# Keeping two more pairs' v on the core in a sorted-block attention followed by a bilinear feed-forward

## The chip, the cores and the metric

The kernel runs on one core of one Trainium2 chip. The metric is the device time of one execution in microseconds. A core has a matrix engine (TensorE, PE in the profile; its weight loads are PEld), VectorE (DVE), ScalarE (ACT), GpSimd (POOL) and SyncE (SP), and 16 DMA engines that move data between DRAM and the on-chip memory. Each engine has its own queue of instructions and works through it in order; they wait for each other through semaphores, which a framework sets from the data dependences. Matrix products land in PSUM, from where VectorE or ScalarE copies them on.

## The reference

The inputs are q, k, v of shape 4 x 8 x 768 x 64 (batch, head, position, head dimension), an 8 x 8 sorting matrix per head, and the three weights of a feed-forward block.

```python
P = sort_net                       # 5 rounds: softmax over rows, then columns divided by their sums
k_sorted = einsum('bhij,bhjcd->bhicd', P, k_b)      # k in 8 blocks of 96 positions
v_sorted = einsum('bhij,bhjcd->bhicd', P, v_b)
scores = scale * q_b @ k_sorted^T  # each block attends to its own sorted block
attn = softmax(scores)
x = (attn @ v_sorted) -> (3072 tokens, 512)
out = ((x @ w_a) * (x @ w_b)) @ w_out               # 512 -> 1536 -> 512
```

The softmax is computed without the subtraction of the maximum, and its sum comes from a column of ones beside v.

## The kernel before

The work is cut into 16 **pairs** g of two heads, four for each batch. A pair goes through these steps:

- **C**: q is transposed on TensorE (`stage_q`, line 173, for the first two batches) or by a DMA (`q_by_dma`); k is mixed with the sorting matrix (`stage_mix`, 12 matmuls, line 186) and copied out of PSUM by ScalarE into one of five buffers kT; v is mixed.
- **R**: the scores of both halves of the blocks (line 234) and their exponentials on ScalarE (eT, line 240).
- **O**: the output matmuls `o_ps` from eT and the sorted v in `vs` (line 262), a reciprocal and a multiplication on VectorE (rec, line 266, and xp, line 268), and a transposing DMA of xp into xT, the input of the feed-forward (`to_xT_dma`, line 294).

v can go two ways. The pairs of batch 0 use `stage_mix` for v, two copies into a buffer vT (`evac_v`), eight transposes on TensorE and one copy into vs (`stage_v`, lines 248 and 250). All other pairs use `stage_v_natural`: two matmuls (line 202), one copy by VectorE (vn, line 161), a write of vn to DRAM (vd, line 208), and later `read_v`, which reads it back into vs in the other order of axes (line 212). vs has three buffers, pair g uses number g mod 3.

The feed-forward of a batch is a list of 72 **slots**: 48 of the products with w_a and w_b (`ffn_mm`, four matmuls of 384 columns, line 306; the results are copied by ScalarE, line 315, and multiplied by VectorE into hT, line 323), then 24 of the output product (`ffn_out`, three matmuls of 512 columns, line 339; every fourth one copies the result to o_sb and sends it out by two DMAs, line 346). The accumulators of the feed-forward rotate through three PSUM banks.

The steps of the pairs of batch b are hung between the slots of the batch ahead of it: `after[s]` lists what is issued behind slot s. The order on TensorE, SP and GpSimd is the order of the program; on ScalarE and VectorE the framework orders the instructions of the main loop itself. For batch 1 the list holds, before:

| pair | C | read of v | R | O |
|---|---|---|---|---|
| 4 | 21 | 27 | 29 | 34 |
| 5 | 31 | 37 | 39 | 44 |
| 6 | 41 | 47 | 49 | 54 |
| 7 | 51 | 57 | 59 | 64 |

From pair 8 on C, read, R and O stand at slots 72(b-1) + 15hp + (-4, 2, 8, 14), hp being the pair's number in its batch.

The loads of k, v and q of pair g + 3 are issued by GpSimd in step C of pair g (`load_pair`, lines 90 and 94), into rings of three buffers, so that each takes the place of pair g's. In the C step of pair 4 the last two thirds of w_out are loaded too. The writes and reads of v, the transposing DMAs and the output's DMAs are all issued by SP, in one queue.

Of the kernel before, what the change touches and what calls it, by code (L numbers as in the profile page):

```python
# [22 lines left out]
def kernel(  # L23
# [11 lines left out]
    nc = tc.nc  # L35
    P = 128
    B, H, S, D = q.shape
# [3 lines left out]
    DMODEL = H * D  # L41
# [5 lines left out]
    HP = H // 2  # L47
# [29 lines left out]


    BD = 2
    BV = 1  # L80

    def load_pair(g):
        b, hp = divmod(g, HP)
# [73 lines left out]
    def copy(eng, out, in_):  # L157
        if eng is nc.scalar:
            nc.scalar.copy(out=out, in_=in_)  # L159
        else:  # L160
            eng.tensor_copy(out=out, in_=in_)  # L161
# [35 lines left out]
    def stage_v_natural(g, pool, tag, eng):  # L197


        mix = pool.tile([P, 2, 512], FP32, tag=tag, name="mix")  # L200
        for e in range(2):
            nc.tensor.matmul(mix[:, e, 0:W], lhsT=s_all[:, 2 * g + e].rearrange("p i c -> p (i c)"),  # L202
                             rhs=loaded[g][1][:, e], start=True, stop=True)
        vn = att.tile([P, NCH, 2, D], BF16, tag="vn", name="vn")
        copy(eng, vn.rearrange("p c e d -> p e c d"),
             _ap(mix, 0, [[1024, P], [512, 2], [D, NCH], [1, D]]))
        vd = drp.tile([P, NCH * 2 * D], BF16, tag="vd", name="vd")
        nc.sync.dma_start(out=vd, in_=vn.rearrange("p c e d -> p (c e d)"))
        st[g, "vd"] = vd
# [6 lines left out]
    def evac_k_natural(g, eng):  # L216
        copy(eng, _ap(kTs[g % NKV], 0, [[S + PAD, P], [NCH, P], [1, NCH]]),
             _ap(st[g, "k"], 0, [[1024, P], [1, P], [P, NCH]]))

    def evac_k(g, eng):  # L220
        copy(eng, _ap(kTs[g % NKV], 0, [[S + PAD, P], [CG, NCH], [BLK, NB], [1, CG]]),
             _ap(st[g, "k"], 0, [[1024, P], [P, NCH], [CG, NB], [1, CG]]))

    def evac_v(g, eng, h):
        copy(eng, _ap(vTs[g % NKV], h * HK, [[2 * HK, P], [CG, NCH], [BLK, NBH], [1, CG]]),
             _ap(st[g, "v"], h * NBH * CG, [[1024, P], [P, NCH], [CG, NBH], [1, CG]]))

    def stage_scores(g, pool, tag, h):
        kT, qT, eT = kTs[g % NKV], st[g, "qT"], eTs[g % NBUF]
        sc = pool.tile([P, 2, 512], FP32, tag=tag, name="sc")  # L230
        for i in range(NBH):
            for e in range(2):
                blk = h * NBH + i
                nc.tensor.matmul(  # L234
                    sc[:, e, i * BLK:(i + 1) * BLK],
                    lhsT=kT[e * D:(e + 1) * D, blk * BLK:blk * BLK + P],
                    rhs=(qT[e * D:(e + 1) * D, blk] if g < BD * HP else
                         qT[e * D:(e + 1) * D, :, blk * CG:(blk + 1) * CG]),
                    start=True, stop=True)
        nc.scalar.activation(out=eT[:, h, :, 0:HB], in_=sc[0:BLK, :, 0:HB],  # L240
                             func=AF.Exp, scale=float(scale))
# [50 lines left out]
    def to_xT_dma(g):  # L292
        xT = xT_of(g // HP)
        nc.sync.dma_start_transpose(
            out=_ap(xT, g % HP * S, [[KA * S, P], [BLK, NB], [1, BLK]]),
            in_=st[g, "xp"].rearrange("q i e d -> q (i e d)"))
# [35 lines left out]
    def ffn_out(b, t, c, part, pool):  # L332
        hT = hTs[b]
        c0 = t * HW + c * P
        if part == 0:
            st[b, t, c] = pool.tile([P, DMODEL], FP32, tag="F", name="po")
        po = st[b, t, c]
        for m in range(part * KO // NPO, (part + 1) * KO // NPO):
            nc.tensor.matmul(po, lhsT=hT[:, m, c0:c0 + P], rhs=w_out_sb[:, m, :],  # L339
                             start=(m == 0), stop=(m == KO - 1))  # L340
        if part < NPO - 1:
            return
        o_sb = ffp.tile([P, DMODEL], FP32, tag="o_sb", name="o_sb", bufs=6)
        copy(nc.scalar if c % 2 == 0 else nc.vector, o_sb, po)
        for u in range(2):
            nc.sync.dma_start(
                out=_ap(out, (b * S + t * NBH * BLK + 2 * c + u) * DMODEL,
                        [[NCH * DMODEL, NBH * CG], [1, DMODEL]]),
                in_=o_sb[u * NBH * CG:(u + 1) * NBH * CG])
# [18 lines left out]
    with tc.manual_schedule(engines={mybir.EngineType.PE, mybir.EngineType.SP,  # L368
# [3 lines left out]
        with tc.manual_schedule(engines=fast), \  # L372
# [7 lines left out]
            for it in range(5):  # L380
# [9 lines left out]
                if it == 0:  # L390
                    with nc.allow_low_precision("sum of one one and zeros"):
                        nc.vector.reduce_sum(
                            out=mask, in_=_ap(ident, 0, [[P, P], [1, CG], [CG, NB]]), axis=AX.X)
# [43 lines left out]
        with tc.tile_pool(name="psA", bufs=2, space=PSUM) as psA, \  # L437
                tc.tile_pool(name="psB", bufs=1, space=PSUM) as psB, \
                tc.tile_pool(name="psF", bufs=3, space=PSUM) as psF:
            def Q1(g):  # L440
                stage_q(g, psA, "A", nc.vector, 1)

            def S1(g):
                stage_scores(g, psA, "A", 1)

            def V1(g):
                stage_v(g, psB, "B", 1)

            def O1(g):
                stage_o(g, psA, "A", 1)  # L450

            def X1(g):
                to_xT(g, psB, "B", 1, nc.vector)

            def C(g):
                if g < BD * HP:
                    stage_q(g, psB, "B", nc.vector)
                stage_mix(g, "k", psA, "A")
                evac_k_natural(g, nc.scalar)
                stage_v_natural(g, psA, "A", nc.vector)  # L460
                if g + 3 < B * HP:
                    load_pair(g + 3)
                if g == BV * HP:
                    for c in range(1, 3):
                        load_out(c)

            def R(g):
                stage_scores(g, psA, "A", 0)
                stage_scores(g, psA, "A", 1)

            def O(g):
                stage_o(g, psA, "A", 0)
                stage_o(g, psA, "A", 1)
                to_xT_dma(g)

            with tc.manual_schedule(engines=fast):
                g = HP - 1
                parts = {}
                for n_, (m, w_sb) in enumerate(((0, w_a_sb), (0, w_b_sb), (1, w_a_sb))):
                    parts[m, w_sb is w_b_sb] = ffn_mm(0, m, 0, w_sb, psF, 0, KA - 1)  # L480
                    if n_ == 0:
                        stage_o(g, psA, "A", 0)
                to_xT(g, psB, "B", 0, nc.vector)
                Q1(0)

            second = {0: [(Q1, 1)], 2: [(S1, 0)], 3: [(V1, 0)], 4: [(S1, 1)],
                      5: [(O1, 0), (V1, 1)], 6: [(Q1, 2)], 7: [(X1, 0)], 8: [(S1, 2), (O1, 1)],
                      9: [(V1, 2)], 10: [(Q1, 3)], 11: [(X1, 1)], 12: [(S1, 3), (O1, 2)],
                      13: [(V1, 3)], 14: [(X1, 2)], 15: [(O1, 3)], 17: [(X1, 3)]}

            NSL = 4 * KO + 2 * 3 * NPO
            after = {s: [] for s in range(-NSL, B * NSL)}
            for s, u in second.items():
                after[s] += u
            for g in range(HP, B * HP):
                b, hp = divmod(g, HP)
                r = (b - 1) * NSL + (29 + 10 * hp if b == 1 else 8 + 15 * hp)
                c_, o_ = r - (8 if b == 1 else 12), r + (5 if b == 1 else 6)
                if b >= BD:
                    after[c_ - 4].append((q_by_dma, g))  # L500
                after[c_ + 6].append((read_v, g))
                after[c_].append((C, g))
                after[r].append((R, g))
                after[o_].append((O, g))
            s = 0
            for b in range(B):
                steps = []
                for m, t in ([(m, t) for t in range(2) for m in range(KO)] if b == 0 else
                             [(m, t) for m in range(KO) for t in range(2)]):
                    for f, u in ((ffn_a, False), (ffn_b, True)):  # L510
                        pf = parts.pop((m, u), None) if (b, t) == (0, 0) else None
                        steps.append(lambda f=f, m=m, t=t, b=b, pf=pf: f(b, m, t, psF, pf))
                for t in range(2):
                    for c in range(3):
                        for part in range(NPO):
                            steps.append(lambda t=t, c=c, part=part, b=b:
                                         ffn_out(b, t, c, part, psF))
                for step in steps:
                    step()
                    for f, g in after[s]:  # L520
                        f(g)
                    s += 1
# [29 lines left out]
```

## Time and profile before

| | |
|---|---|
| median of 3 runs | 259.35 us (259.15 to 260.0) |
| profiled execution | 258.78 us |
| its span, first to last instruction | 257.0 us |
| mean granted clock of TensorE | 0.987 |
| TensorE busy | 239.6 us (93%) |
| VectorE busy | 114.5 us (45%) |
| ScalarE busy | 97.9 us (38%) |
| GpSimd busy | 55.9 us (22%) |

In the groups of the profile a line gives the line of the kernel, the engine, the operation, output and inputs with their shapes and the count; behind the bar stand the busy time in us and the mean duration in ns, and behind the second bar the idle time of the engine just ahead of these instructions with what ended it. In the list of waits a line gives who waited, for whom, the total in us, the number of waits and the longest. In the chain of waits in order of time, and in the timeline, a line begins with the start in us and the duration; the chain names what set the end at each moment. vs_116, vs_117 and vs_118 are the three buffers of vs, used by pairs 0, 3, 6, ..., by 1, 4, 7, ... and by 2, 5, 8, ...

### The profile page before, as it was taken

How to read it: one execution, taken by the hardware profiler on the slowest of the kernel's cores; microseconds unless marked ns; L12 is line 12 of the kernel's file. 1: busy time of each engine (PE TensorE's matmuls, PEld its weight loads, DVE VectorE, ACT ScalarE, POOL GpSimd, SP SyncE). 2: the span in 40 equal slices, each digit the busy share in tenths (PEclk: the TensorE clock that was granted, in tenths of full speed). 3: DMA queues.
4: the chain of work that ended last, by engine and by line, in shares of the span. 5: the costliest groups of instructions: out<-in, count | busy, mean ns of one | idle time of the engine just before them, and what ended most of it. 6: DMA issues, size and time to landing. Idle time of an engine off the chain costs nothing.

```text
span 257.0 us, 5119 instructions
## 1 busy us (share of the span) xinstructions
PE 239.6 (93%) x2068; PEld 135.8 (53%) x2081; DVE 114.5 (45%) x260; ACT 97.9 (38%) x176; POOL 55.9 (22%) x75
## 2 busy tenths in 40 slices
PE   8888999974999879999999999999999999999992
PEld 3465665642555345656564455656555466655440
DVE  6766676542365052565471233746443134444110
ACT  3484542450433413635543135462623043333010
POOL 8494383540044013304040040000000000000000
PEclk9999999996899999999999999999999999999999
DMA  6999998799298949995968599152553520000243
GB/s 90 197 203 203 203 201 128 112 181 152 61 137 119 209 112 187 130 173 74 158 101 126 117 141 195 39 87 72 53 93 86 132 59 3 0 0 3 50 113 82
DMA packets 60247, 29.44 MB, mean 115 GB/s; under 512 B 39744, under 2 KB 57152, under 8 KB 60224
## 3 DMA queue, kind: packets, MB, share of 16 engines
q0 software_dynamic: 29200, 14.16, 43.8%
q1 hardware_dynamic: 31024, 14.96, 29.7%
q8 instruction: 16, 0.26, 0.4%
q14 instruction: 7, 0.06, 0.1%
HBM read 30.68 MB, written 8.65 MB: 153 GB/s over the span
## 4 chain that ended last, share of the span: by engine, by line
PE 77%; DMA 10%; DVE 2%; issue 1%; ACT 0%; SPq 0%
PE pf L306 46%; PE po L339 21%; DMA vs_117<-vd 5%; DMA vd<-vn 4%; PE o_ps L262 3%; PE sc L234 2%; PE mix L202 2%; PE mix L186 2%; PE q_ps L173 1%; DVE vn L161 1%; PE xt_ps L287 1%; PE vs_ps L248 0%; DVE xp L268 0%; ACT o_sb L159 0%; DVE hT L323 0%
## 5 line engine op out<-in xcount | busy, mean ns | idle before, releaser
L323 DVE TENSOR_TENSOR hT<-a_sb,pf 128x384 bf16<-128x384 bf16 x96 | 53.2, 554 | 67.8 <-PE pf L306 55.8
L306 PE MATMUL pf<-xT,w_a_sb 128*128 128x384 bf16 x384 | 79.3, 329 | 0.8 <-DVE xT L161 0.7
L306 PE MATMUL pf<-xT,w_b_sb 128*128 128x384 bf16 x384 | 79.7, 330 | 0.0
L315 ACT CAST a_sb<-pf 128x384 bf16<-128x384 f32 x96 | 46.0, 479 | 82.4 <-DVE hT L323 50.2
L339 PE MATMUL po<-w_out_sb,hT 128*128 128x512 bf16 x276 | 63.0, 379 | 0.6 <-issue 0.2
L306 PEld LDWEIGHTS <-w_a_sb 128*128 128x128 bf16 x384 | 37.0, 99 | 25.0 <-issue 2.0
L306 PEld LDWEIGHTS <-w_b_sb 128*128 128x128 bf16 x384 | 36.6, 99 | 23.7 <-issue 1.0
L339 PEld LDWEIGHTS <-hT 128*128 128x128 bf16 x288 | 27.6, 98 | 31.7
L159 ACT COPY o_sb<-po 128x512 f32<-128x512 f32 x16 | 9.4, 586 | 44.1 <-PE po L339 38.7
L268 DVE TENSOR_TENSOR xp<-o_ps,rec 96x512 bf16<-96x512 f32 x32 | 21.7, 684 | 0.7
L161 DVE COPY o_sb<-po 128x512 f32<-128x512 f32 x8 | 5.5, 686 | 29.3 <-PE po L339 25.6
L266 DVE RECIPROCAL rec<-o_ps 96x8 f32<-96x8 f32 x32 | 6.1, 197 | 24.0 <-PE o_ps L262 22.8
L161 DVE CAST vn<-mix 128x768 bf16<-128x768 f32 x12 | 11.5, 956 | 4.4 <-PE mix L202 4.2
L262 PE MATMUL o_ps<-vs_117,eT_114 96*128 96x65 bf16 x80 | 4.0, 204 | 7.4 <-DMA vs_117<-vd 7.4
L365 PE MATMUL w_ps<-warm_sb 128*128 128x512 bf16 x32 | 9.4, 448 | 1.4 <-DVE warm_sb L71 1.2
L240 ACT ACTIVATE eT_113<-sc 96x768 bf16<-96x768 f32 x12 | 9.3, 805 | 3.3 <-PE sc L234 3.2
L240 ACT ACTIVATE eT_115<-sc 96x768 bf16<-96x768 f32 x10 | 7.6, 805 | 1.4 <-PE sc L234 1.4
L262 PEld LDWEIGHTS <-eT_114 96*128 96x128 bf16 x80 | 3.4, 104 | 8.7 <-DMA vs_117<-vd 5.6
L240 ACT ACTIVATE eT_114<-sc 96x768 bf16<-96x768 f32 x10 | 7.6, 806 | 0.9 <-PE sc L234 0.9
L355 POOL TENSOR_TENSOR s_all<-mask,p_col 128x1024 bf16<-128x1024 bf16 (+1 forms) x5 | 7.2, 1457 | 3.4 <-ACT p_col L408 3.4
L365 PEld LDWEIGHTS <-warm_sb 128*128 128x128 bf16 x33 | 3.3, 111 | 5.6 <-issue 2.5
L161 DVE COPY qT<-q_ps 128x384 bf16<-128x384 bf16 (+1 forms) x8 | 3.6, 453 | 3.5 <-PE q_ps L173 3.4
(192 smaller groups left out, 161.5 us busy)
## 6 DMA issues: line engine op xcount, KB each, us to landing
out_dram<-o_sb SPq DMA_DIRECT2D x48, 128.0 KB, 2.4
vd<-vn SPq DMA_DIRECT2D x12, 192.0 KB, 4.6
w_a_sb<-in_moe_w_a_dram POOLq DMA_DIRECT2D x4, 384.0 KB, 9.7
w_b_sb<-in_moe_w_b_dram POOLq DMA_DIRECT2D x4, 384.0 KB, 11.1
w_out_sb<-in_moe_w_out_dram POOLq DMA_DIRECT2D x3, 512.0 KB, 7.9
q_first<-in_q_dram POOLq DMA_DIRECT2D x2, 384.0 KB, 6.0
vs_117<-vd SPq DMA_DIRECT2D x4, 192.0 KB, 4.1
vs_118<-vd SPq DMA_DIRECT2D x4, 192.0 KB, 3.8
```

The lines of the kernel that those rows point to most:

```text
L159: nc.scalar.copy(out=out, in_=in_)
L161: eng.tensor_copy(out=out, in_=in_)
L240: nc.scalar.activation(out=eT[:, h, :, 0:HB], in_=sc[0:BLK, :, 0:HB], func=AF.Exp, scale=float(scale))
L262: nc.tensor.matmul(o_ps[:, e, i * (D + 1):(i + 1) * (D + 1)], lhsT=eT[:, h, e, i * BLK:i * BLK + P], rhs=vs[:, h * NBH + i, e * (D + 1):(e ...
L266: nc.vector.reciprocal(out=rec, in_=_ap(o_ps, 0, [[1024, BLK], [512 + D, 2], [D + 1, NBH]]))
L268: nc.vector.tensor_tensor(out=_ap(xp, h * NBH * 2 * D, [[NB * 2 * D, BLK], [D, 2], [2 * D, NBH], [1, D]]), in0=_ap(o_ps, 1, [[1024, BLK], ...
L306: nc.tensor.matmul(pf[:, 0:HW], lhsT=w_sb[:, kc, m * P:(m + 1) * P], rhs=xTs[b][:, kc, t * HW:(t + 1) * HW], start=(kc == 0), stop=(kc == ...
L315: nc.scalar.copy(out=a_sb, in_=pf[:, 0:HW])
L323: nc.vector.tensor_tensor(out=_ap(hTs[b], m * S + t * HW, [[KO * S, P], [CG, NBH], [NBH * CG, NCH], [1, CG]]), in0=st[b, m, t].rearrange(" ...
L339: nc.tensor.matmul(po, lhsT=hT[:, m, c0:c0 + P], rhs=w_out_sb[:, m, :], start=(m == 0), stop=(m == KO - 1))
L355: eng.tensor_tensor(out=s_all[:, h0:h0 + n], in0=_ap(mask, 0, [[CG, P], [0, n], [0, NB], [1, CG]]), in1=_ap(src, h0, [[NB * BH, P], [1, n] ...
L365: nc.tensor.matmul(w_ps[:, 0:cols], lhsT=warm_sb[:, 0:P], rhs=warm_sb[:, 0:cols], start=True, stop=True)
```

## The change

Three things change.

1. Pairs 4 and 5 take v the way that batch 0 does (mixing, two copies to vT by VectorE, eight transposes in step R, one copy to vs); `GV = 6` is the first pair whose v goes through DRAM. Their k is copied to kT in the other order of columns, to fit. The slots of the four pairs of batch 1 are now written out one by one:

| pair | C | read of v | R | O |
|---|---|---|---|---|
| 4 | 22 | none | 27 | 32 |
| 5 | 30 | none | 36 | 41 |
| 6 | 34 | 42 | 47 | 53 |
| 7 | 39 | 49 | 55 | 62 |

The slots of pairs 8 to 15 stay as they were.

2. The loads of pairs 8 to 15 stand in the program behind step O of pair g instead of in its step C. The load of pair 7 and of w_out stays in the C step of pair 4.

3. The very last output tile is copied out of PSUM in two halves of 256 columns, one by ScalarE, one by VectorE, instead of whole by ScalarE.

```diff
-    BV = 1
+    GV = 6
...
-        copy(nc.scalar if c % 2 == 0 else nc.vector, o_sb, po)
+        if (b, t, c) == (B - 1, 1, 2):
+            nc.scalar.copy(out=o_sb[:, 0:DMODEL // 2], in_=po[:, 0:DMODEL // 2])
+            nc.vector.tensor_copy(out=o_sb[:, DMODEL // 2:], in_=po[:, DMODEL // 2:])
+        else:
+            copy(nc.scalar if c % 2 == 0 else nc.vector, o_sb, po)
...
                 stage_mix(g, "k", psA, "A")
-                evac_k_natural(g, nc.scalar)
-                stage_v_natural(g, psA, "A", nc.vector)
-                if g + 3 < B * HP:
+                if g >= GV:
+                    evac_k_natural(g, nc.scalar)
+                    stage_v_natural(g, psA, "A", nc.vector)
+                else:
+                    evac_k(g, nc.scalar)
+                    stage_mix(g, "v", psA, "A")
+                    for h in range(2):
+                        evac_v(g, nc.vector, h)
+                if g == HP:
                     load_pair(g + 3)
-                if g == BV * HP:
                     for c in range(1, 3):
                         load_out(c)
...
                 stage_scores(g, psA, "A", 1)
+                if g < GV:
+                    stage_v(g, psB, "B")
...
                 to_xT_dma(g)
+                if HP < g < B * HP - 3:
+                    load_pair(g + 3)
...
-                r = (b - 1) * NSL + (29 + 10 * hp if b == 1 else 8 + 15 * hp)
-                c_, o_ = r - (8 if b == 1 else 12), r + (5 if b == 1 else 6)
+                if b == 1:
+                    c_, v_, r, o_ = ((22, 0, 27, 32), (30, 0, 36, 41), (34, 42, 47, 53),
+                                     (39, 49, 55, 62))[hp]
+                else:
+                    c_, v_, r, o_ = ((b - 1) * NSL + 15 * hp + u for u in (-4, 2, 8, 14))
...
-                after[c_ + 6].append((read_v, g))
+                if g >= GV:
+                    after[v_].append((read_v, g))
```

## The prediction

> **What bounds the kernel now.** I read the page's head first, then the waits of TensorE, then the chain of waits in order of time, then the busy time of two stretches.
>
> The engines' row, TensorE's waits and the page's clock row:
>
> ```profile
> span 257.0 us, 5119 instructions
> PE 239.6 (93%) x2068; PEld 135.8 (53%) x2081; DVE 114.5 (45%) x260; ACT 97.9 (38%) x176; POOL 55.9 (22%) x75
> PEclk9999999996899999999999999999999999999999
> PE o_ps L262 <- DMA vs_117<-vd: 7.4, 2, 5.2
> PE w_ps L365 <- DVE warm_sb L71: 1.2, 1, 1.2
> ```
>
> TensorE (PE) is the bound at 93%. Of its waits one group counts: the output matmuls of stage o (line 262) wait twice for v to come back from DRAM, 7.4 us together; the next one, 1.2 us, is at the start. Two slices of the clock row fall to 6 and 8 tenths. The chain shows where the two waits are:
>
> ```profile
> 45.11 0.34 PE mix L186 x12
> 45.45 0.45 PE mix L202 x2
> ...
> 46.90 4.81 DMA vd<-vn
> ...
> 51.79 9.46 DMA vs_117<-vd
> ...
> 61.29 1.06 PE o_ps L262 x16
> 62.35 5.30 PE pf L306 x20
> 67.65 0.45 PE sc L234 x16
> ...
> 70.73 1.95 PE pf L306 x12
> 72.68 0.52 PE o_ps L262 x16
> ...
> 80.54 6.14 DMA vd<-vn
> ...
> 86.73 4.39 DMA vs_117<-vd
> ...
> 143.28 5.83 PE po L339 x27
> ```
>
> A slot of the main loop is four matmuls pf or three po: 1.95 / 3 = 0.65 us, and 5.83 / 9 the same. The first trip is that of pair 4 (write 4.81 us, read 9.46 us), the second that of pair 7 (6.14 and 4.39). Behind the first wait 20 matmuls of the feed-forward take 5.30 us, where 12 take 1.95 later: 0.27 against 0.16 us each, so the clock is gone too. Busy time by stretch (columns: stretch, length, PE, PE loads, DVE, ACT, POOL, granted clock, DMA share, GB/s):
>
> ```profile
> 56.10:61.29 5.19, 0.00 (x1) 0.00 (x0) 0.01 (x1) 0.48 (x1) 0.96 (x2) 0.83 1.28 210
> 61.29:66.39 5.10, 5.10 (x30) 2.90 (x31) 2.24 (x6) 0.48 (x1) 0.00 (x0) 0.50 0.57 45
> 88.00:91.26 3.26, 1.01 (x6) 0.30 (x4) 0.00 (x0) 0.59 (x1) 0.00 (x0) 1.00 1.15 298
> ```
>
> PE stands still for 5.19 us, then works 5.10 us at half clock. The second idle time, 3.26 - 1.01 = 2.25 us, costs no clock.
>
> **Pairs 4 and 5 without DRAM.** Pair 4's wait cannot be there any more: its v never leaves the core. Gone: 5.19 us of idle time and, as half-clock work is worth half its time, 5.10 x 0.5 = 2.55 us.
>
> What comes in its place, per pair: the mixing matmuls of v like those of k (12, 0.34 us) instead of the two natural ones (0.45): -0.11. Then eight transposes in stage R, at the rate of the row below, 0.22 us for four: +0.44. For two pairs: 2 x (0.44 - 0.11) = **+0.66 us** on PE, which has no idle time left there to hide it in.
>
> ```profile
> 33.97 0.22 PE vs_ps L248 x4
> ```
>
> A rule of the Trainium skill speaks against this: its page TensorE: Matmul & The Clock Gate, Part 4, gives about 275 ns for one 128x128 transpose in a kernel, as such a transpose does not get the full clock. By that, an estimate from the page, 16 transposes would be 4.4 us instead of 0.9 and the gain some 3.5 us smaller. The row has 0.055 us each in the same kernel between the same matmuls, so I keep it.
>
> **VectorE and ScalarE.** Durations (busy, mean ns):
>
> ```profile
> L323 DVE TENSOR_TENSOR hT<-a_sb,pf 128x384 bf16<-128x384 bf16 x96 | 53.2, 554 | 67.8 <-PE pf L306 55.8 <-ACT a_sb L315 6.2 <-ACT eT_115 L240 2.6
> L268 DVE TENSOR_TENSOR xp<-o_ps,rec 96x512 bf16<-96x512 f32 x32 | 21.7, 684 | 0.7
> L161 DVE CAST vn<-mix 128x768 bf16<-128x768 f32 x12 | 11.5, 956 | 4.4 <-PE mix L202 4.2
> L266 DVE RECIPROCAL rec<-o_ps 96x8 f32<-96x8 f32 x32 | 6.1, 197 | 24.0 <-PE o_ps L262 22.8 <-issue 1.2
> L161 DVE COPY qT<-q_ps 128x768 bf16<-128x768 bf16 x4 | 2.2, 553 | 3.0 <-PE q_ps L173 3.0
> L250 DVE COPY vs_116<-vs_ps 96x512 bf16<-96x512 bf16 x4 | 1.7, 415 | 0.0
> L161 DVE CAST vT_109<-mix 128x384 bf16<-128x384 f32 x1 | 0.6, 558 | 0.0
> L159 ACT CAST kT_103<-mix 128x768 bf16<-128x768 f32 x4 | 3.2, 799 | 1.3 <-PE mix L186 1.3
> 32.00:38.00 6.00, 6.00 (x80) 3.71 (x78) 4.21 (x11) 2.85 (x5) 5.05 (x4) 1.00 1.31 200
> ```
>
> The k evacuation changes its order but not its size; the row's four, pairs 0, 5, 10 and 15, have both orders and one mean of 799 ns: 0. VectorE gets two halves of vT (2 x 0.558) for one vn (0.956), and one vs copy of double width (between 0.415 and 0.83; I take 0.83): +0.99 us a pair.
>
> That matters because the four pairs now stand closer. From the C step of pair 4 (slot 22) to the O step of pair 5 (slot 41) PE does 20 slots of 0.65 us (13.0), four C steps (two of 0.46 + 0.34 + 0.34, two of 0.46 + 0.34 + 0.45; 0.46 is the row of the q transposes below), two R steps (0.45 + 0.44) and two O steps (0.52): 20.6 us. VectorE has in it 10 hT (5.5), 4 qT (2.2), 4 vT (2.2), 2 vs (1.7), 2 vn (1.9) and 4 of rec and xp (3.5): 17.0 us, a share of 83%. The densest stretch of 6 us shown above has 4.21 of 6 (70%), with PE never idle. I followed the queue slot by slot with these durations: hT is at most 1.5 us late (behind O of pair 4), and three PSUM buffers for the feed-forward cover about that. I charge **+0.2 us**; bounds 0 and 3.8 (below).
>
> **Pair 6: the next thing that can be late.** Its v still goes through DRAM. The read is issued by SP, whose queue is in order: write of pair 6, write of pair 7, transpose of pair 5's xp, read of pair 6, read of pair 7. So the read cannot start before pair 5's O step is through VectorE, although its place is only one slot behind that. Before, the order around pair 6's read was the same:
>
> ```profile
> 72.52 0.68 PE L262 MATMUL o_ps<-vs_118,eT_115 96*128 96x65 bf16 x16
> 75.14 1.23 SPq L294 DMA_TRANSPOSE xT<-xp  x1
> 76.52 0.47 SPq L212 DMA_DIRECT2D vs_116<-vd  x1
> 81.30 0.68 PE L262 MATMUL o_ps<-vs_116,eT_113 96*128 96x65 bf16 x16
> DMA to landing us min/median/max: 3.5/3.9/4.1
> 69.51 0.46 PE q_ps L173 x12
> ```
>
> The read was issued 76.52 - 72.52 = 4.0 us after pair 5's O step and landed at most 4.1 later (the row of transfers to this buffer), 8.1 in all; pair 6's O step came 81.30 - 72.52 = 8.78 us after pair 5's. After the change: 0.52 + 12 slots (7.8) + the scores of pair 6 (0.45) = 8.77. The same slack, 0.7 us. What is new is the traffic: the loads of pairs 8, 9 and 10 (192 KB each for k, v, q) fall into fewer microseconds, and a read beside loads has taken 4.39 (pair 7) and, beside the weights, 9.46 (pair 4). At 4.39 there is still no wait; at 9.46 the wait is 4.0 + 9.46 - 8.77 = 4.7 us, near the 5.19 that cost the clock and far from the 2.25 that did not, so 7.2 with 2.55 for it. (The Trainium skill, TensorE: Matmul & The Clock Gate, Part 1, lets the clock drop after about 3.4 us of idle time; by that too the 4.7 us would cost it.) I take **+0.3 us**, since pair 6's own row and pair 7's are nearest in what runs beside them. Pair 7: its O step moves to slot 62, 13 slots behind its read's place; at 0.65 that is 8.5 us against 4.39. Its write, 6.14 us, is issued near slot 40 and done well before that; pair 6's, issued about 1.0 us (vn) behind slot 34, has 7 slots, R of pair 5, C of pair 7 and the 4.0 us, 9.7 us in all, before its read. So the 2.25 us are gone as well.
>
> **Loads moved to the O step.** What released such a load:
>
> ```profile
> POOL k_1264 L94 <- PE mix L186: 13.5, 1, 13.5
> k_312<-in_k_dram POOLq DMA_DIRECT2D x1, 192.0 KB, 13.3
> ```
>
> GpSimd stood 13.5 us before that load, until pair 6's mixing had let its buffer go. It has nothing else to do there, so a later place in the program behind no other GpSimd work moves nothing: the load will still start when mixing ends. Price 0. Should it start at the O step after all, pair 8 has from slot 41 to slot 64, 23 x 0.65 = 15 us, against 13.3 us, the longest landing of any transfer on the page: also 0.
>
> **The last tile.** Its copy (128x512) stands alone at the end:
>
> ```profile
> L159 ACT COPY o_sb<-po 128x512 f32<-128x512 f32 x16 | 9.4, 586 | 44.1 <-PE po L339 38.7 <-remote 5.3
> L161 DVE COPY o_sb<-po 128x512 f32<-128x512 f32 x8 | 5.5, 686 | 29.3 <-PE po L339 25.6 <-DMA out_dram<-o_sb 3.7
> ```
>
> VectorE's 384 columns at 558 and 512 at 686 make 1.0 ns a column, so 256 take 0.43; ScalarE's half is shorter. 0.59 - 0.43 = **-0.16 us**; bounds -0.24 (half of 686) and +0.1 (686 whole).
>
> **The sum.** -5.19 - 2.55 - 2.25 + 0.66 + 0.2 + 0.3 - 0.16 = **-9.0 us**. The profiled execution took 258.78 us (span 257.0, 1.8 around it): 249.8. The median of the runs, 259.35, lies 0.57 higher, which I carry over: **250.3 us**.
>
> **Rivals.** (1) The stall moves to pair 6. For it: a slack of 0.7 us, loads packed closer, the 9.46. Against: 3.5 to 4.1 on this buffer. With a read between 6 and 9.46 us the loss is 1.2 to 7.2 us on 250.0: 251.2 to 257.2. Chance 0.17. (2) VectorE becomes the bound of the dense stretch. If it cannot be kept above 70%, its 17.0 us need 24.3 instead of 20.6: +3.7, so 253.8. Against: the arithmetic above, with all its lateness inside the PSUM buffers. Chance 0.08. (3) Slower: pair 6's read waits as long as the longest transfer of the trace, 13.3 us (k of pair 4 behind the first weights). Its wait is then 4.0 + 13.3 - 8.77 = 8.5 us, 11.1 with the clock, against a gain of 9.3 without the 0.3: 261. It decides from a read of about 11.5 us on; no weights are left to load by then, so 0.02. (4) The added transposes run at half rate, as stage o did at half clock (1.06 us for 0.52): +0.9 us, 251.2; the 0.22 us row speaks against it; 0.02. The page on the clock gate quoted above is the one that would have it so. (5) Nothing changes, because another wait stands right behind those removed: PE's list of waits has none; 0.02. The forecast, with at most 1.2 us of new waits, keeps 0.69.
>
> A difference of 0.3% (0.8 us) is what this kernel's timing can tell from none. Faster by more: forecast, (2), (4) and nearly all of (1): 0.95; same 0.03; slower 0.02. The range runs from 249.0 (no new wait, no 0.57) up to 253.8, which leaves out the upper part of (1) and (3), some 0.15 together, and takes in (2).
>
> **What would show it.** No wait of o_ps for the buffers of pairs 4 and 5, the clock row at 9 throughout, DVE near 83% between slots 22 and 41. Pair 6's read issued about 4 us behind pair 5's O step. k loads still released by mixing. Wrong, if PE shows a new wait of over 1.2 us, most likely at pair 6's O step, or many short ones on hT.

## The result, and the profile after

The changed kernel takes **252.39 us** in the median of four runs (251.68 to 253.88); the kernel before took 259.25 beside it. The ratio is **0.9737**, 95% interval 0.9684 to 0.9791. The profiled execution took 251.68 us, 7.10 us less than that of before (258.78); the forecast was 9.0 less there and a median of 250.3. The direction and the range hold; 2 of the 9 us did not come.

The page's head, the engines' row and the clock row, then TensorE's waits, of the changed kernel:

```profile
span 249.9 us, 5205 instructions
PE 238.5 (95%) x2117; PEld 136.0 (54%) x2117; DVE 116.1 (46%) x265; ACT 97.5 (39%) x176; POOL 55.9 (22%) x75
PEclk9999999999999999999999999999999999999999
PE o_ps L262 <- DMA vs<-vd: 1.4, 1, 1.4
PE w_ps L369 <- DVE warm_sb L71: 1.2, 1, 1.2
```

The two waits of 7.4 us are gone, and so is the dip of the clock. One new wait of stage o for DRAM stands in their place. The chain of waits in order of time (start, duration, what) shows whose it is:

```profile
45.23 0.46 PE q_ps L173 x12
45.68 0.67 PE mix L186 x24
46.35 3.36 PE pf L306 x20
49.71 0.45 PE sc L234 x16
50.15 0.55 PE vs_ps L248 x8
...
55.19 0.52 PE o_ps L262 x16
...
65.00 0.52 PE o_ps L262 x16
65.52 2.93 PE pf L306 x19
68.45 6.68 DMA vs<-vd
75.13 0.14 issue
75.27 0.68 PE o_ps L262 x16
75.94 1.30 PE po L339 x6
77.24 0.30 PE sc L234 x8
77.54 0.01 issue
77.55 0.34 PE sc L234 x8
...
244.82 0.38 ACT o_sb L345
245.20 0.02 issue
245.23 0.42 DVE o_sb L346
```

Pairs 4 and 5 (O steps at 55.19 and 65.00) do not wait. Pair 6's read is issued at 68.45 and takes 6.68 us; its O step starts at 75.27, 1.41 us late. Behind it the scores of pair 7 come in two pieces, 0.65 us instead of 0.45. The end shows something else that was not foreseen: the two halves of the last tile are copied one behind the other. From the last matmul to the end of the second half it is 0.85 us; with the whole copy of before it was 0.62.

### The profile page after: what moved, and what is told of

Read it like the earlier page. It is cut to its first block, busy times and chain, and to the rows that moved or that the text cites. A ratio compares the mean times of both kernels' runs of the same rounds, so it can differ in the third digit from the quotient of the medians.

```text
span 249.9 us, 5205 instructions
## 1 busy us (share of the span) xinstructions
PE 238.5 (95%) x2117; PEld 136.0 (54%) x2117; DVE 116.1 (46%) x265; ACT 97.5 (39%) x176; POOL 55.9 (22%) x75
## 4 chain that ended last, share of the span: by engine, by line
PE 85%; DMA 3%; DVE 1%; issue 1%; ACT 0%
PE pf L306 49%; PE po L339 23%; PE o_ps L262 3%; DMA vs<-vd 3%; PE sc L234 2%; PE mix L186 2%; PE mix L202 2%; PE q_ps L173 1%; PE vs_ps L248 1%; PE xt_ps L287 1%; DVE xp L268 0%; DVE hT L323 0%; DVE o_sb L346 0%; ACT o_sb L345 0%; DVE xT L161 0%
## 5 line engine op out<-in xcount | busy, mean ns | idle before, releaser
L306 PE MATMUL pf<-xT,w_b_sb 128*128 128x384 bf16 x384 | 78.4, 326 | 0.0
L240 ACT ACTIVATE eT<-sc 96x768 bf16<-96x768 f32 x32 | 24.5, 805 | 8.2 <-PE sc L234 8.2
L94 POOL DMA_DIRECT2D k<-in_k_dram x12 | 8.4, 700 | 76.0 <-PE mix L186 72.5
L159 ACT CAST kT<-mix 128x768 bf16<-128x768 f32 x16 | 12.8, 798 | 11.8 <-PE mix L186 11.7
L90 POOL DMA_DIRECT2D q<-in_q_dram x16 | 13.1, 821 | 3.4 <-DMA qT<-q 3.2
L262 PE MATMUL o_ps<-vs,eT 96*128 96x65 bf16 x256 | 11.6, 194 | 1.5 <-DMA vs<-vd 1.4
L262 PEld LDWEIGHTS <-eT 96*128 96x128 bf16 x256 | 10.5, 98 | 4.5 <-issue 1.9
L161 DVE CAST vn<-mix 128x768 bf16<-128x768 f32 x10 | 9.6, 958 | 4.4 <-PE mix L202 4.2
L234 PE MATMUL sc<-qT,kT 64*128 64x96 bf16 x256 | 9.1, 204 | 0.7 <-ACT kT L159 0.6
L234 PEld LDWEIGHTS <-kT 64*128 64x128 bf16 x256 | 6.0, 94 | 6.9 <-issue 5.0
```

Source lines behind the costliest of these rows:

```text
L90: nc.gpsimd.dma_start(out=_ap(to, e * D, [[2 * W, P], [2 * D, NCH], [1, D]]), in_=_ap(t, at + e * S * D, [[W, P], [D, NCH], [1, D]]))
L234: nc.tensor.matmul(sc[:, e, i * BLK:(i + 1) * BLK], lhsT=kT[e * D:(e + 1) * D, blk * BLK:blk * BLK + P], rhs=(qT[e * D:(e + 1) * D, blk] i ...
L262: nc.tensor.matmul(o_ps[:, e, i * (D + 1):(i + 1) * (D + 1)], lhsT=eT[:, h, e, i * BLK:i * BLK + P], rhs=vs[:, h * NBH + i, e * (D + 1):(e ...
L306: nc.tensor.matmul(pf[:, 0:HW], lhsT=w_sb[:, kc, m * P:(m + 1) * P], rhs=xTs[b][:, kc, t * HW:(t + 1) * HW], start=(kc == 0), stop=(kc == ...
```

## The experiments

Each kernel is the changed one with the edit shown. "Profiled" is the time of its profiled execution. The first matmul of the feed-forward starts at 22.78 us in the trace of the changed kernel and at 22.81 to 23.40 in those below, though no edit changes what stands ahead of it, so two profiled times can differ by up to 0.6 us for that alone.

**The changed kernel once more.**

> The changed kernel once more, unaltered. Its first four runs lay between 251.68 and 253.88 us, with a mean granted clock between 1.0 and 0.99. Theory A (the wait of pair 6's O step for its v, 1.41 us in the profile, is of differing length from run to run and sometimes costs the clock as well): again 251.5 to 254, the runs with the lower clock being the longer ones by about what the clock lost; if the profiled run is one of these, the clock falls right behind pair 6's O step. Rival B (the clock is lost elsewhere, such as at the start): the same spread, but the fall stands at another place.

Median 251.99 us (251.93 to 254.76), ratio 0.9724 [0.9651, 0.9797]. Pair 6's wait was again 1.4 us in the profiled execution (252.00 us) and the clock stood at full throughout. The long run, 254.76, was not the profiled one, so no trace shows where it lost 2.8 us. A mean clock of 0.995 tells little: a run with it took 251.98 us and one at 1.0 took 252.00. (The trace of the last kernel of this section, with a mean of 0.995, has its only fall at 245.45 us, 2.2 us behind the last matmul.) What the spread comes from is taken up by the next runs.

**Pair 6's O step later, and earlier.**

```diff
-                    c_, v_, r, o_ = ((22, 0, 27, 32), (30, 0, 36, 41), (34, 42, 47, 53),
+                    c_, v_, r, o_ = ((22, 0, 27, 32), (30, 0, 36, 41), (34, 42, 47, 56),
```

> Only pair 6's O step moves, from slot 53 to slot 56, which gives its read 1.95 us more against a wait of 1.41. Theory A: the wait is gone, the scores of pair 7 no longer wait behind it (0.2 us), profiled time near 250.1 us, all runs within 0.5 us of each other with a clock of 0.999 or more, median near 250.2, 2 us below the changed kernel's. Rival B: the profiled time falls by 1.5 us as well, but runs with a lower clock stay and the median falls by 1.5 us at most. Rival C (the wait only moves on to pair 7's O step or to the start of batch 1's feed-forward): no gain.

Median 250.67 us, ratio 0.9638 [0.9599, 0.9677], and all four runs between 250.58 and 250.70. The wait for DRAM is gone from TensorE's list (0.3 us for pair 7's exponentials came in, since the O step now stood right behind them). Its profiled execution, 250.58 us, is 1.1 us shorter than that of the changed kernel; 250.1 had been expected, and the 0.3 us is part of the difference. The spread goes with the wait, which speaks for theory A: the range shrinks from 2.2 us to 0.12.

```diff
-                    c_, v_, r, o_ = ((22, 0, 27, 32), (30, 0, 36, 41), (34, 42, 47, 53),
+                    c_, v_, r, o_ = ((22, 0, 27, 32), (30, 0, 36, 41), (34, 42, 47, 50),
```

> Pair 6's O step three slots earlier (50 instead of 53): its wait for the read grows by 1.95 us, from 1.4 to 3.3. This doubles the disputed wait and asks what it costs with the clock. If the clock holds: 251.68 + 1.95 = 253.6 profiled, median near 254. If a wait of this length already costs the clock, as the 5.19 us before did: up to 2.5 us more, 254 to 256.5, with a stretch at half clock behind the wait. The longest runs of the changed kernel, 253.9 and 254.8, would be explained by waits of this size.

Median 255.47 us (254.80 to 256.53), ratio 0.9836 [0.9796, 0.9875]. Its wait line and three stretches of its trace (stretch, length, PE, PE loads, DVE, ACT, POOL, clock, DMA share, GB/s):

```profile
PE o_ps L262 <- DMA vs<-vd: 3.0, 1, 3.0
...
72.20:75.23 3.03, 0.01 (x1) 0.03 (x1) 0.00 (x0) 0.00 (x0) 0.00 (x0) 0.94 1.38 122
75.23:78.25 3.02, 3.02 (x22) 1.65 (x23) 1.69 (x4) 0.59 (x1) 0.00 (x0) 0.50 0.02 6
78.25:81.00 2.75, 2.75 (x28) 1.31 (x27) 0.41 (x1) 0.13 (x1) 0.00 (x0) 1.00 0.65 137
```

The wait grew by 1.6 us, and 3.0 us of standing still were enough to lose the clock: half speed until 78.25, 3.02 us of work at half, so 1.5 us more. Together 3.1 us; the profiled execution is 3.12 us longer, 254.80 against 251.68, though 0.3 us of that came ahead of the feed-forward. In this trace the granted clock is 0.50 from 74.84 to 78.25 us, 3.41 us long. In the kernel before, it is 0.50 from 59.56 to 66.39 us, 6.83 us and twice that; the first 1.7 us of it lie inside the wait. The Trainium skill (TensorE: Matmul & The Clock Gate, Part 1) has a window of 3413 ns for this; both lengths agree with it. So a wait of pair 6 that is only 1.6 us longer costs twice that, and the longest runs of the changed kernel, 2.2 and 2.8 us above the shortest, are of the size that this gives. Their mean clocks, 0.990 and 0.992, leave room for one such piece, which is 0.007 of the mean. That it was this in those runs is argued, not shown.

**Loads that really wait for the O step.** The loads' new place in the program did nothing: in the changed kernel's timeline GpSimd still issues each k load when the mixing of pair g ends (11 to 19 us ahead of its O step):

```profile
53.75 0.70 POOL L94 DMA_DIRECT2D k<-in_k_dram  x1 [3.81 <-PE mix L186]
58.10 0.70 POOL L94 DMA_DIRECT2D k<-in_k_dram  x1 [1.33 <-PE mix L186]
63.59 0.70 POOL L94 DMA_DIRECT2D k<-in_k_dram  x1 [2.41 <-PE mix L186]
```

To hold them, GpSimd was made to read a column of xp first:

```diff
                 if HP < g < B * HP - 3:
+                    hold = att.tile([BLK, 1], BF16, tag="hold", name="hold")
+                    nc.gpsimd.tensor_copy(out=hold, in_=st[g, "xp"][:, NB - 1, 1, D - 1:D])
                     load_pair(g + 3)
```

> GpSimd first reads one column of pair g's xp, so that the loads of pair g + 3 really begin behind pair g's O step, not when the mixing of pair g frees their buffers. Theory A1 (pair 6's read is late because the write of pair 7, the transpose of pair 5's xp and the read of pair 6 follow each other in SP's ring, and the write is held up by the loads of pairs 8 to 10): the write of pair 7 lands in about 4.5 us instead of over 5, pair 6's wait falls below 0.4 us, time near 250.3. Rival A2 (the read itself is slowed by loads that run beside it): the load of pair 8 now runs beside the read, which takes 6 us or more, and the wait stays at 1 to 3 us, time 251.5 to 254. Moved loads that were without effect in the changed kernel: there the k loads start when the mixing ends, here 2 us behind the O step.

Median 252.63 us (251.68 to 252.94), ratio 0.9707 [0.9664, 0.9751]: no gain over the changed kernel. DMA issues between 57 and 77 us (size, then median us from issue to landing), first the changed kernel, then this one:

```profile
vd<-vn SPq DMA_DIRECT2D x2, 192.0 KB, 6.3
...
vs<-vd SPq DMA_DIRECT2D x2, 192.0 KB, 6.5
...
xT<-xp SPq DMA_TRANSPOSE x2, 6.3
```

```profile
vd<-vn SPq DMA_DIRECT2D x2, 192.0 KB, 1.9
vs<-vd SPq DMA_DIRECT2D x2, 192.0 KB, 6.9
...
xT<-xp SPq DMA_TRANSPOSE x2, 3.6
```

The writes fell from 6.3 to 1.9 us and the transposes from 6.3 to 3.6, as A1 had it, and the read did not move, as A2 had it (6.51 us for pair 6): now the load of pair 8 ran beside it. The wait at pair 6 was 1.24 us, and pair 9 waited 0.5 us more, for a read of 8.18 us. So A1 alone is not the cause.

**Pair 6's read ahead of the transpose.**

```diff
-                    c_, v_, r, o_ = ((22, 0, 27, 32), (30, 0, 36, 41), (34, 42, 47, 53),
+                    c_, v_, r, o_ = ((22, 0, 27, 32), (30, 0, 36, 41), (34, 40, 47, 53),
```

> Only the place of pair 6's read moves, from slot 42 to slot 40, which puts it ahead of the transposing DMA of pair 5's xp in SP's queue. In the changed kernel the read landed 2.0 us behind that transpose (73.10 and 75.13) and 6.7 us after its own issue. Theory A1 (the ring works them off one behind the other): the read lands about 2 us behind the write of pair 7 (70.2), near 72.5, pair 6's O step (due at 73.9) does not wait, profiled time 251.68 - 1.6 = 250.1, median near 250.3 with little spread; the transpose lands 2 us later, near 75, which nothing needs. Rival A2 (the read is slow by the loads beside it, wherever it stands): it lands near 74.5 to 75, wait 0.7 to 1.2 us, time 251 to 252.

Median 251.01 us (250.24 to 252.5), ratio 0.967 [0.9621, 0.9719]. No wait for DRAM in the profiled execution, but not by A1's way: the read, issued 0.6 us earlier, still took 6.47 us and landed at 74.34, just as the O step fell due at 74.37; 72.5 had been expected. It could not be issued earlier either, as it waits for pair 6's own write, which landed at 67.79. The order in the queue alone does not make the read fast, and with no time to spare the runs still lay 2.3 us apart.

**Loads neither ahead of the read nor beside it.**

```diff
+                if g == GV:
+                    hold = att.tile([BLK, 1], BF16, tag="hold", name="hold")
+                    nc.gpsimd.tensor_copy(out=hold, in_=eTs[g % NBUF][:, 1, 1, HB - 1:HB])
+                    load_pair(g + 2)
...
-                if HP < g < B * HP - 3:
+                if GV - 1 < g < B * HP - 3:
+                    hold = att.tile([BLK, 1], BF16, tag="hold", name="hold")
+                    nc.gpsimd.tensor_copy(out=hold, in_=st[g, "xp"][:, NB - 1, 1, D - 1:D])
                     load_pair(g + 3)
```

> As the kernel whose loads wait for the O step, but the load of pair 8 is held until the exponentials of pair 6 (some 71 us after the start, 2.5 us behind the issue of pair 6's read), that of pair 9 until pair 6's O step and so on. Now neither the write of pair 7 nor loads stand before or beside the read. Theory E (the read is slow by either: by what is ahead of it in the ring, and by loads beside it): the read takes 3.5 to 4.5 us instead of 6.7, no wait at pair 6's O step, profiled 250.1 to 250.4; should pair 8's q come too late for its transposing DMA (slot 64), a wait at pair 8's R step would show instead. Rival F (the read is slow by the read of pair 7 right behind it in the ring): it still takes 6 us or more and the wait stays at 1.2 to 1.5.

Median 250.57 us (250.11 to 251.17), ratio 0.9648 [0.9604, 0.9693]; profiled 250.11 us. No wait at pair 6, nor at pair 8. Issues between 57 and 77 us:

```profile
vd<-vn SPq DMA_DIRECT2D x2, 192.0 KB, 1.9
vs<-vd SPq DMA_DIRECT2D x2, 192.0 KB, 4.7
...
xT<-xp SPq DMA_TRANSPOSE x3, 2.9
```

Pair 6's read took 4.48 us, with pair 7's still right behind it: F falls. Against the kernel whose loads waited for the O step, only the loads moved, and the read fell from 6.51 us to 4.48: loads beside it are enough to slow it. Whether loads ahead of it would do that alone, the other half of E, no run tells, since none has them ahead and not beside. The DMA page of the Trainium skill (DMA: Bandwidth & Descriptors, Issuing engines are not separate DMA queues) says that transfers of all issuing engines run on the same 16 DMA engines and interleave. The rows agree: the same 192 KB write takes 1.9 us without loads beside it and 6.3 with them.

**What each part is worth.** First pairs 6 and 7 on the core as well:

```diff
-    GV = 6
+    GV = 8
```

> Pairs 6 and 7 also keep v on the core (GV = 8), so batch 1 has no trip through DRAM at all. Theory A: wait of 1.41 and the 0.2 behind it gone, for two more pairs 0.46 us of TensorE work each (0.55 for eight transposes, 0.09 less for mixing): 251.68 - 1.6 + 0.9 = 251.0 in the profile, all runs within 0.5 us, clock 0.999 or more, median about 251. Rival D (VectorE becomes the bound, as its share in the dense stretch rises by 2 us in 21): new waits of TensorE for VectorE of 1 us or more, 252 or above. Rival B: the spread of the runs stays.

Median 251.10 us (250.98 to 251.43), ratio 0.9657 [0.9617, 0.9697]; profiled 251.43 us. That is 0.4 above theory A's 251.0, and the feed-forward began 0.4 us later than in the changed kernel; TensorE has no wait for VectorE that the changed kernel has not. The price of the way on the core is in line with 0.46 us of TensorE work a pair, and the runs are steady again. Then the old slots:

```diff
-                    c_, v_, r, o_ = ((22, 0, 27, 32), (30, 0, 36, 41), (34, 42, 47, 53),
-                                     (39, 49, 55, 62))[hp]
+                    c_, v_, r, o_ = ((21, 0, 29, 34), (31, 0, 39, 44), (41, 47, 49, 54),
+                                     (51, 57, 59, 64))[hp]
```

> The changed kernel with the four pairs of batch 1 at the slots that they had before (C 21, 31, 41, 51; read of pairs 6 and 7 at 47 and 57; R 29, 39, 49, 59; O 34, 44, 54, 64), so that pairs 4 and 5 without DRAM is what remains, beside the last tile and the loads. By the sum: 5.19 of wait and 2.55 of clock gone, 0.92 of new TensorE work, 0.24 for the last tile, and pair 7's 2.25 us stays, as its write and read stand as before: 258.78 - 7.74 + 0.92 + 0.24 = 252.2 profiled. Rival: the new slots carry part of the gain from pair 4 too, or pair 6 now waits: 253.5 or more. Rival: pair 7's wait was a consequence of the stall ahead of it and goes with it: 250.

Median 251.95 us (251.84 to 253.09), ratio 0.9706 [0.9668, 0.9744]; profiled 251.84 us (expected 252.2). The new slots were worth nothing that these runs can tell. In the old ones pair 7 waits instead of pair 6:

```profile
PE o_ps L262 <- DMA vs<-vd: 1.5, 1, 1.5
...
73.88 0.62 SPq L208 DMA_DIRECT2D vd<-vn  x1
77.31 1.25 SPq L294 DMA_TRANSPOSE xT<-xp  x1
78.61 1.22 SPq L350 DMA_DIRECT2D out_dram<-o_sb  x2
79.94 0.52 SPq L212 DMA_DIRECT2D vs<-vd  x1
```

Here the read itself is fast (3.77 us, 79.94 to 83.71), but it comes late. Pair 7's write, issued at 73.88 beside loads, landed only at 79.30, and the read waits for it; issued right then, it would still have made the O step wait some 0.9 us. The other 0.6 us are SP's queue, where two output DMAs stand ahead of the read. It is the same stall with another cause.

**The last tile whole again.**

```diff
-        if (b, t, c) == (B - 1, 1, 2):
-            nc.scalar.copy(out=o_sb[:, 0:DMODEL // 2], in_=po[:, 0:DMODEL // 2])
-            nc.vector.tensor_copy(out=o_sb[:, DMODEL // 2:], in_=po[:, DMODEL // 2:])
-        else:
-            copy(nc.scalar if c % 2 == 0 else nc.vector, o_sb, po)
+        copy(nc.scalar if c % 2 == 0 else nc.vector, o_sb, po)
```

> Only the last output tile is copied whole by ScalarE again. In the changed kernel VectorE's half began when ScalarE's had ended (0.37 and 0.42 us one behind the other, 0.81 from the last matmul on, against 0.59 before). Theory: the halves stand in a row, so undoing them gives 0.2 us back: profiled near 251.5, the copy 0.59 us behind the last matmul. Rival (as the prediction had it: the halves run side by side and save 0.16): undoing them costs 0.16. The times alone cannot tell 0.2 us with the spread of the changed kernel's runs; the trace's end can.

Median 252.20 us of six runs (250.95 to 253.55), ratio 0.9706 [0.9669, 0.9743]: pair 6's wait is still in it and its spread hides 0.2 us. The profiled execution took 252.00 us, not 251.5, as its feed-forward began 0.6 us later. The ends of the two traces tell it, first the changed kernel's timeline, then this kernel's chain:

```profile
244.82 0.37 ACT L345 COPY o_sb<-po 128x256 f32<-128x256 f32 x1 [4.59 <-PE po L339]
245.23 0.42 DVE L346 COPY o_sb<-po 128x256 f32<-128x256 f32 x1 [2.30 <-ACT o_sb L345]
```

```profile
229.83 15.55 PE po L339 x72
245.38 0.02 issue
245.41 0.59 ACT o_sb L159
```

VectorE waited for ScalarE: the program has it wait on ScalarE's semaphore there. Whether the framework sets that for the shared output tile or for the shared PSUM bank was not tried.

**A version that beats both.** Pair 6's O step at 56 without exponentials right ahead of it, and the last tile whole:

```diff
-                    c_, v_, r, o_ = ((22, 0, 27, 32), (30, 0, 36, 41), (34, 42, 47, 53),
-                                     (39, 49, 55, 62))[hp]
+                    c_, v_, r, o_ = ((22, 0, 27, 32), (30, 0, 36, 41), (34, 42, 47, 56),
+                                     (39, 49, 53, 62))[hp]
...
-        if (b, t, c) == (B - 1, 1, 2):
...
+        copy(nc.scalar if c % 2 == 0 else nc.vector, o_sb, po)
```

> The changed kernel with pair 6's O step at slot 56, pair 7's R step at slot 53 (so that the O step does not stand right behind exponentials, which cost it 0.3 us), and the last tile copied whole by ScalarE. From the kernel with pair 6's O step at 56 alone (250.58 profiled): -0.3 - 0.2 = 250.1, no wait of TensorE over 0.3 us behind the first 45 us, runs within 0.5 us. Rival: pair 7's exponentials, now ahead of pair 6's O step, or the later O step make a new wait: 250.5 or above.

Median **249.84 us** of six runs (249.81 to 250.46), ratio 0.9625 [0.9586, 0.9664]; profiled 249.81 us. Its chain around pair 6:

```profile
69.98 3.99 PE po L339 x18
73.98 0.45 PE sc L234 x16
74.42 2.05 PE po L339 x9
76.47 0.52 PE o_ps L262 x16
76.99 3.02 PE po L339 x14
```

TensorE goes through without a gap, though the read took 7.40 us here (68.57 to 75.97): it has 0.5 us to spare. With pair 6's read at slot 40 besides (`(34, 40, 47, 56)`):

> The same, and pair 6's read at slot 40, ahead of the transposing DMA of pair 5. If the read is in time at slot 56 in either order, this makes no difference: 250.1, as the kernel beside it. A slack of 1.3 us more for the read shows only in its landing (near 74.3 instead of 76).

Median 249.80 us (249.76 to 249.96), ratio 0.9618 [0.9575, 0.9662], the same time; the read landed at 73.31, which is 2.7 us earlier than in the kernel beside it and 1.0 earlier than expected. It was issued at 66.86, as soon as pair 6's write had landed (66.78). By that landing it is the safer order.

## Why the prediction was right, and where it was not

The direction was right, by the mechanism that the prediction named, and the time lay in its range. But its own sign of being wrong, a new wait of over 1.2 us at pair 6's O step, came: what happened is rival (1), which had a chance of 0.17, and not the forecast. That the range held it is in part luck, as its upper end was set by rival (2), which did not come. Term by term, on the profiled executions (-9.0 forecast, -7.10 measured):

- **Pair 4's wait and the clock, pair 7's wait** (-5.19, -2.55, -2.25): right. All three are gone from the waits and the clock row. The old slots show that keeping pairs 4 and 5 on the core does nearly all of it; that pair 7's 2.25 us went by new slots was right in the letter, but in the net the slots gave nothing, as pair 6 took over 1.41 us.
- **TensorE's new work** (+0.66): mis-sized, it was +0.9. Eight transposes in a row take 0.55 us, not twice the 0.22 of four; that makes 2 x (0.55 - 0.11). Rival (4) falls. The record of a single transpose is 219 ns long here, but in a row they overlap and cost 0.069 us each. So the about 275 ns that the Trainium skill (TensorE: Matmul & The Clock Gate, Part 4) gives for one was not the price of one more in a row.
- **VectorE** (+0.2): no wait of TensorE for it came. Its share between 45.23 and 67.10 us, pair 4's C step to the end of pair 5's xp, was 15.64 of 21.87 us, 72% and not 83% (columns as before, VectorE's is the third busy time):

```profile
45.23:67.10 21.87, 21.87 (x291) 14.57 (x292) 15.64 (x32) 11.25 (x19) 12.70 (x17) 1.00 1.22 157
```

All the copies and products of the sum are in it, but the vs copy took 0.69 us and not 0.83, and records that follow each other at once overlap a little (two vT halves of 0.56 us take 1.02 together). The stretch is longer than the 20.6 us of the sum because the work of the last O step ends 1.6 us behind TensorE's.

- **Pair 6's read** (+0.3): the step that failed. The forecast took the read for 4.1 to 4.4 us, by pair 6's own row of before and pair 7's; it measured 6.68, between these and the 9.46 of the read beside the weights. The read was issued 3.45 us behind pair 5's O step, earlier than the 4.0 of the sum; its length alone used up the slack. The wait of 1.41, the 0.2 behind it and a slower start of the O step (0.68 for 0.52) make 1.8 us. This is rival (1), which began at a read of 6 us and a loss of 1.2; its kernel time of 251.2 to 257.2 holds all eight runs of the changed kernel. The cause that the forecast named, the loads of pairs 8 to 10 packed closer, is shown by the last of the load experiments: without them beside the read and ahead of it, 4.48 us and no wait. The old slots fit: there these loads run from 54.7 to 80.7 us, not from 53.8 to 72.0, and the same read took 3.67 us. What the prediction had not seen is that the same loads also hold up the writes, for which the reads wait, and the transposes.
- **The loads' place** (0): right, shown by GpSimd's rows. The alternative, had they really begun at the O step, was also put at 0; with pair 6's wait it gave nothing, so that holds too.
- **The last tile** (-0.16): wrong in sign, +0.23 (0.85 for 0.62 us). The halves were taken to run side by side; they ran in a row.
- **The median** (+0.57 over the profiled execution): it came out 0.7 over it, but by another way: not an even offset but single long runs. They are shorter or gone where the read has time to spare.

With the measured sizes the sum is -9.99 + 0.88 + 0 + 1.77 + 0.23 = -7.1 us, the -7.10 measured.

Rivals (3) and (5) did not come; rival (2) is answered by VectorE's 72% and by the run with pairs 6 and 7 on the core as well, which loads it more and showed no wait.

## What to carry to other kernels

Taking a stall away moves the end to the next transfer with little slack; price that one by the rows of transfers that ran beside the traffic it will meet, not by its own row in quieter company, and give it a few slots more than its usual length needs. A load's place in the program is not its time: on a queue that holds nothing else it starts when its buffer comes free, and holding it back takes a real dependence. Two engines that copy halves of one tile are worth nothing until the trace shows them side by side.

## What the hardware showed unexpectedly

A wait of 3.0 us cost the clock (1.41 and 2.25 us did not), and the loss came in one piece of 3.41 us at half speed; the wait of 5.19 us before had cost two such pieces. No fixed length of idle time decides it: the clock fell 3.46 us into the wait of 5.19 us and 2.6 us into that of 3.0 us, and behind the last matmul it fell after 2.2 us in one trace and after 4.9 us in the changed kernel's. So a wait of 2.25 us that cost nothing in one trace is no safe length.

With the new slots a 192 KB write to DRAM of pair 6 or 7 took 1.8 to 2.0 us without loads and 5.2 to 8.8 us beside GpSimd's loads. Pair 6's read, in runs of 256 bytes, took 3.7 to 4.5 us in the kernels where few or no loads ran beside it and 6.3 to 7.5 in the others. Where it landed too late or with nothing to spare, the runs of one kernel lay 1.3 to 2.8 us apart; with 0.4 to 0.8 us to spare 0.1 to 1.1 us, and with some 3 us to spare 0.2 us.
